# The last four gradient stores of an attention backward pass, each issued as nine transfers over every ninth partition

## The chip, the cores and the metric

The kernel runs on one core of a Trainium2 chip. Its time is device microseconds for one execution of the whole program. The median of the runs before the change is 1698.76 us (three runs, 1698.05 to 1699.05). One more execution was recorded by the hardware profiler; its span, from the first to the last instruction, is 1696.2 us, so the span is 2.6 us shorter than the median time. All sums are made on the profiled execution, and differences are carried over to the median.

## What is computed

The reference runs one decode step of a transformer block forward (attention over a key and value cache, then a gated feed-forward layer) and returns its output and the gradients of all inputs but one. Cut to what matters here:

```
q = (x @ wq) as B=4 batches x H=32 heads x Dh=128
p = softmax(q . k_cache / sqrt(Dh))          # k_cache: 4 x 32 x 4096 x 128
o = p . v_cache
...
dV[b,h] = outer(p[b,h], do[b,h])             # 4096 x 128 for each of the 128 heads
dK[b,h] = outer(ds[b,h], q[b,h])             # the same shape
```

Each head's dK and dV is an outer product of a vector with 4096 elements and one with 128, so there is little arithmetic and much to store: dK and dV are 128 heads x 1 MB each. With the two passes over the caches the page counts 422.59 MB read and 282.34 MB written.

## The kernel before the change

All engines' instruction streams are written out by hand order (`tc.manual_schedule()`, line 98); a framework adds the semaphore waits that the data dependences need. One large SBUF tile, `arena` (line 112), is cut into 23 slots of 4160 bf16 elements in each of the 128 partitions. `Slot` takes one, `Slot2` (line 146) takes two neighbours, enough for a pair of heads, 128 partitions x 8192 elements (16 KB a partition, 2 MB). `give` puts slots back on the list when the transfer that reads them has been issued; the framework makes the next writer wait until that transfer has landed.

The work has three phases: a forward pass over all heads, the feed-forward layer, and the backward pass. In the backward pass the last 96 heads go as 48 pairs (`NT = 48`). For each pair t the loop of line 1476 does the following:

- `load_pairs` (line 1282) loads v for a later pair (line 1280);
- `front_pair` (line 1292) transposes v with TensorE (line 1298), copies it back with ScalarE (line 1299) and multiplies it with do (line 1313);
- `more_V` (line 1395) makes dV of some pair: `P2_pair` on GpSimd (line 1376), then `grad_pair` into `out_3` (line 1414);
- `grad_pair` into `out_2` (line 1489) makes dK of pair t;
- after every second pair `group_dS_pair` (line 1319, with lines 1326 and 1329 on VectorE) makes the ds of the next two.

`grad_pair` (line 1386) takes a slot pair, runs one VectorE product of 128 x 8192 (line 1379), and issues one store of 2 MB from SyncE's queue (line 1389). In DRAM the two heads of a pair are next to each other, and `two_heads` (line 1272) views them as 128 rows of 8192 elements, one for each partition.

All large loads and stores go through SyncE's queue in the order of the program. The framework gives them eight completion semaphores in turn, called lanes here: a transfer waits, before it is issued, until the one eight places earlier in the queue has landed completely. A semaphore counts to 16 for each transfer.

The last four products of the program are, in this order on VectorE: dK of pair 45, dV of pair 47, dK of pair 46, dK of pair 47.

Of the kernel before, what the change touches and what calls it, by code (L numbers as in the profile page):

```python
# [27 lines left out]
def kernel(  # L28
# [22 lines left out]
    nc = tc.nc  # L51
# [6 lines left out]
    Dh = A_k_cache.shape[3]  # L58
# [6 lines left out]
    SJ = Sk // P  # L65
# [142 lines left out]
    for i in range(2):  # L208
        t = fcon.tile([P, 64], BF16, name=f"onesw{i}")
# [4 lines left out]
    def ones_window(col):  # L214
# [11 lines left out]
                          in_=rowg[:, None, :, None].to_broadcast([P, 4, 8, 4]))  # L226
# [738 lines left out]
    with ExitStack() as c2:  # L965
# [297 lines left out]
        NT = (NH - SP) // 2  # L1263
# [8 lines left out]
        def two_heads(ap, t):  # L1272
            b, h = t % B, H0 + t // B * 2
            return ap[b, h:h + 2].rearrange("h (p j) d -> (h p) (j d)", p=P // 2)
# [103 lines left out]
        def outer_pair(dst, col2, row):  # L1378
            nc.vector.tensor_tensor(  # L1379
                out=dst.rearrange("p (j r t) -> p j r t", r=Dh // 2, t=2),  # L1380
                in0=col2[:, :, None, :].to_broadcast([P, 2 * SJ, Dh // 2, 2]),
                in1=row.rearrange("p (r t) -> p r t", t=2)[:, None, :, :].to_broadcast([P, 2 * SJ, Dh // 2, 2]),
                op=ALU.mult,
            )

        def grad_pair(out_ap, t, col2, row):
            g_ = Slot2()
            outer_pair(g_.t[:, 0:2 * SJ * Dh], col2, row)
            nc.sync.dma_start(out=two_heads(out_ap, t), in_=g_.t[:, 0:2 * SJ * Dh])
            g_.give()  # L1390

        O0, S0, S1, L, LP = 2, 21, 35, 5, 3
        gvd = {"n": 2, "t": 0}

        def more_V(upto):
            while gvd["n"] < min(SP, upto):
                s = gvd["n"]
                P_pairs(s)
                replicate("rdo", s - s % REP)
                grad_V(s)  # L1400
                P_pairs(s + 1)
                P_pairs(s + 2)
                gvd["n"] += 1
                if s % REP == 2 and s + 2 < SP:
                    replicate("rdo", s + 2)
                elif s % REP == 2:
                    replicate_pair("rdo", 0)
                if s >= SP - 2:
                    P2_pair(s - SP + 2)
            while gvd["t"] < NT and SP + 2 * gvd["t"] + 2 <= upto:  # L1410
                t = gvd["t"]
                P2_pair(t)
                replicate_pair("rdo", t // B)
                grad_pair(out_3, t, pP2.pop(t), reps["rdo", "p", t // B][:, t % B, :])
                P2_pair(t + 1)
                gvd["t"] += 1
                if t % B == 2:
                    replicate_pair("rdo", t // B + 1)
# [57 lines left out]
        for t in range(NT):  # L1476
            s = SP + 2 * t
            load_pairs(t + LP)
            if t % B == 2:
                replicate_pair("rq", t // B + 1)  # L1480
            if t + LP < NT:
                front_pair(t + LP, lambda: side(s))
            else:
                if t + LP == NT:
                    rows_out()
                    rows_T()
                side(s)
            more_V(s + 2 + lead_V(s))
            grad_pair(out_2, t, pdS[t // 2][:, t % 2], reps["rq", "p", t // B][:, t % B, :])
            if t % 2 == 1 and t + 1 < NT:  # L1490
                group_dS_pair((t + 1) // 2)
            side(s + 1)
# [31 lines left out]
```

## Time and profile before

| | |
|---|---|
| median of 3 runs | 1698.76 us (1698.05 to 1699.05) |
| span of the profiled execution | 1696.2 us |
| busy: TensorE, VectorE, ScalarE, GpSimd | 1233.4, 1234.4, 959.5, 336.9 us |
| moved by DMA | 707.45 MB, mean 417 GB/s |
| stores of line 1389 | 96 of 2048 KB, median 27.9 us from issue to landing |
| last product of VectorE ends | 1666.8 us |
| last store issued | 1666.8 us |
| last store landed | 1694.9 us |

The page gives busy shares of each engine; an engine with a low share is not the bound, and one with a high share need not be it either. The DMA row of the page is the mean busy share of the core's 16 DMA engines in 40 slices of the span, a tenth a digit. A stretch can also be asked for alone; a share of 0.06 there is one engine of sixteen (0.0625). The trace also holds every count of every semaphore, so that it can be seen when each of the engines of one transfer was done.

### The profile page before, as it was taken

The page shows a single profiled execution, that of the slowest core. Times are in us where ns is not written, and L with a number is a line of the kernel's source. Part 1 is how long each engine was busy: PE and PEld are TensorE (multiplying, and loading weights), DVE is VectorE, ACT ScalarE, POOL GpSimd, SP SyncE. Part 2 cuts the span into 40 slices and gives each one's busy share as a digit, 9 for nine tenths or more (in the row PEclk, how much of TensorE's full clock was granted, in tenths as well). Part 3 has the DMA queues.
Part 4 walks back from the last instruction along what each step waited for, and adds up shares of the span by engine and source line. Part 5 has one row for each costly group of instructions (what it writes and reads, how often), then busy time and mean ns, then how long its engine had stood idle before and what let it go on. Part 6 is the DMA issues. An engine that isn't in the chain of part 4 may idle for free.

```text
span 1696.2 us, 37839 instructions
## 1 busy us (share of the span) xinstructions
PE 1233.4 (73%) x16228; PEld 943.4 (56%) x16228; DVE 1234.4 (73%) x1198; ACT 959.5 (57%) x1490; POOL 336.9 (20%) x583
## 2 busy tenths in 40 slices
PE   5889888888888888877876755667665666766650
PEld 4777667666677666655655544444444444444440
DVE  5989999999998997667766466575665655655683
ACT  3555544454454544677665555666665666666650
POOL 1211222222222222222231121011210102011120
PEclk8999999999999999899898689886678777676675
DMA  9999999999999999999999999999999999999995
GB/s 401 424 424 424 424 424 424 424 424 423 416 423 406 424 414 397 395 414 425 425 425 429 428 429 428 429 430 429 429 429 428 418 430 429 422 418 425 415 429 230
DMA packets 81000, 707.45 MB, mean 417 GB/s; under 512 B 8748, under 2 KB 12984, under 8 KB 15296
## 3 DMA queue, kind: packets, MB, share of 16 engines
q1 hardware_dynamic: 80416, 704.94, 99.0%
q8 instruction: 127, 2.08, 0.5%
q14 instruction: 41, 0.34, 0.0%
q0 software_dynamic: 416, 0.10, 0.0%
HBM read 422.59 MB, written 282.34 MB: 416 GB/s over the span
## 4 chain that ended last, share of the span: by engine, by line
DMA 46%; DVE 9%; PE 3%; issue 2%; ACT 1%; DVEq 0%; POOL 0%; SPq 0%; ACTq 0%
DMA out_dram<-arena 43%; DVE arena L1379 7%; DMA arena<-in_A_v_cache_dram 3%; DVE arena L806 1%; PE M_ps L472 1%; DVE arena L457 1%; PE pt_w L601 0%; ACT arena L1299 0%; ACT Pn L436 0%; DVEq L1519 0%; PE kP_ps L482 0%; DVE dPr L1326 0%; PE pt_tps L1298 0%; PE gu_ps L873 0%; PE dn_ps L904 0%
## 5 line engine op out<-in xcount | busy, mean ns | idle before, releaser
L1299 ACT COPY arena<-pt_tps 128x1024 bf16<-128x1024 bf16 x384 | 369.8, 1023 | 232.3 <-PE pt_tps L1298 231.6
L1298 PE MATMUL pt_tps<-ident_b,arena 128*128 128x128 bf16 x3072 | 308.1, 272 | 204.7 <-DMA arena<-in_A_v_cache_dram 149.4
L1298 PEld LDWEIGHTS <-arena 128*128 128x128 bf16 x3072 | 263.9, 125 | 304.2 <-DMA arena<-in_A_v_cache_dram 172.8
L1379 DVE TENSOR_TENSOR arena<-arena 128x8192 bf16<-128x8192 bf16 x48 | 212.5, 4427 | 205.1 <-DMA out_dram<-arena 202.3
L472 PE MATMUL M_ps<-arena 128*128 128x130 bf16 x4096 | 285.1, 222 | 42.9 <-DMA arena<-in_A_v_cache_dram 42.2
L457 DVE TENSOR_TENSOR arena<-arena 128x4096 bf16<-128x4096 bf16 x128 | 292.5, 2285 | 23.9 <-POOL arena L453 23.9
L472 PEld LDWEIGHTS <-arena 128*128 128x128 bf16 x4096 | 251.9, 99 | 64.0 <-DMA arena<-in_A_v_cache_dram 57.2
L1379 DVE TENSOR_TENSOR arena<-dS,arena 128x8192 bf16<-128x8192 bf16 x48 | 212.3, 4424 | 73.0 <-DMA out_dram<-arena 73.0
L364 DVE STREAM_TRANSPOSE arena<-arena 128x512 f32<-128x512 f32 (+1 forms) x321 | 250.7, 797 | 0.0
L359 ACT COPY arena<-pt_tps 128x1024 bf16<-128x1024 bf16 x128 | 129.5, 1012 | 188.9 <-PE pt_tps L358 150.5
L1376 POOL COPY arena<-arena 128x128 bf16<-128x128 bf16 x48 | 55.3, 1153 | 492.3 <-ACT arena L1353 286.3
L370 POOL TENSOR_TENSOR W<-qrep,wmask 128x128 bf16<-128x128 bf16 x128 | 120.2, 939 | 85.6 <-PE S_ps L390 70.8
L801 ACT COPY arena<-pt_tps 128x1024 bf16<-128x1024 bf16 x128 | 121.7, 1025 | 26.1 <-PE pt_tps L800 24.8
L453 POOL COPY arena<-P_all 128x64 bf16<-128x64 bf16 x128 | 32.7, 255 | 412.8 <-ACT P_all L447 409.8
L806 DVE TENSOR_TENSOR arena<-dS,arena 128x4096 bf16<-128x4096 bf16 x32 | 73.2, 2293 | 35.0 <-DMA out_dram<-arena 34.7
L800 PE MATMUL pt_tps<-ident_b,arena 128*128 128x128 bf16 x1024 | 78.5, 229 | 27.1 <-ACT arena L801 27.1
L1313 PE MATMUL dP_ps<-arena 128*32 128x512 bf16 x768 | 85.7, 484 | 7.6 <-ACT arena L1299 7.3
L800 PEld LDWEIGHTS <-arena 128*128 128x128 bf16 x1024 | 67.2, 104 | 37.5 <-issue 35.9
L447 ACT COPY P_all<-pt_P 32x64 bf16<-32x64 bf16 x256 | 52.1, 204 | 53.6 <-PE pt_P L443 51.4
L806 DVE TENSOR_TENSOR arena<-P,arena 128x4096 bf16<-128x4096 bf16 x29 | 66.4, 2295 | 19.8 <-DMA out_dram<-arena 19.8
L358 PE MATMUL pt_tps<-ident_b,arena 128*128 128x128 bf16 x1024 | 80.1, 222 | 0.0
L482 PE MATMUL kP_ps<-arena,onesw 128*32 128x512 bf16 x1024 | 79.6, 388 | 0.0
(245 smaller groups left out, 1576.5 us busy)
## 6 DMA issues: line engine op xcount, KB each, us to landing
out_dram<-arena SPq DMA_DIRECT2D x96, 2048.0 KB, 27.9
arena<-in_A_v_cache_dram SPq DMA_DIRECT2D x160, 1024.0 KB, 15.9
arena<-in_A_k_cache_dram SPq DMA_DIRECT2D x128, 1024.0 KB, 15.3
arena<-in_A_v_cache_dram SPq DMA_DIRECT2D x48, 2048.0 KB, 32.1
out_dram<-arena SPq DMA_DIRECT2D x72, 1024.0 KB, 20.2
arena<-in_A_wq_dram SPq DMA_DIRECT2D x8, 1024.0 KB, 14.4
arena<-in_B_w_dram SPq DMA_DIRECT2D x8, 896.0 KB, 15.3
out_dram<-arena SPq DMA_DIRECT2D x6, 896.0 KB, 28.4
```

Of the source, the lines that this page charges most:

```text
L359: nc.scalar.copy(out=KT[:, c * GW:(c + 1) * GW, :], in_=pt[:])
L364: nc.vector.transpose(out=KT[:, c * w_:(c + n) * w_], in_=Kn[:, c * w_:(c + n) * w_])
L370: nc.gpsimd.tensor_tensor(out=W[:, hl], in0=qrep[:, :, s:s + 1].to_broadcast([P, 4, 32]), in1=wmask[:, hl, None, :].to_broadcast([P, 4, 32 ...
L457: nc.vector.tensor_tensor(out=PK[:, :, 0:Dh].rearrange("p j (r t) -> p j r t", t=2), in0=Ks[s].heads().rearrange("p j (r t) -> p j r t", t=2),
L472: nc.tensor.matmul(hold["M"][:], lhsT=Vn[:, j, :], rhs=PK[:, j, :], start=(j == 0), stop=(j == SJ - 1))
L800: nc.tensor.transpose(pt[:, i, :], v[:, g * GW + i, :], ident_b[:])
L801: nc.scalar.copy(out=v[:, g * GW:(g + 1) * GW, :], in_=pt[:])
L806: nc.vector.tensor_tensor(out=dst.rearrange("p j (r t) -> p j r t", t=2), in0=col2[:, :, None, :].to_broadcast([P, SJ, Dh // 2, 2]), in1=r ...
L1298: nc.tensor.transpose(pt[:, i, :], v[:, g * GW + i, :], ident_b[:])
L1299: nc.scalar.copy(out=v[:, g * GW:(g + 1) * GW, :], in_=pt[:])
L1313: nc.tensor.matmul(rows["acc"][32 * c:32 * (c + 1), :], lhsT=zt[t % B][:, 32 - m:64 - m], rhs=v[:, j0:j0 + 4, :], start=(pl == 0 and u == ...
L1379: nc.vector.tensor_tensor(out=dst.rearrange("p (j r t) -> p j r t", r=Dh // 2, t=2), in0=col2[:, :, None, :].to_broadcast([P, 2 * SJ, Dh / ...
```

## The change

The last four stores of pairs (dK of pairs 45, 46 and 47, dV of pair 47) go through a new function. It issues nine transfers in place of one: the first takes partitions 0, 9, 18 and so on to 126, the second 1, 10, ..., 127, and so on. The first two have 15 partitions, the other seven 14. All other stores are issued as before.

```diff
         def grad_pair(out_ap, t, col2, row):
             g_ = Slot2()
             outer_pair(g_.t[:, 0:2 * SJ * Dh], col2, row)
-            nc.sync.dma_start(out=two_heads(out_ap, t), in_=g_.t[:, 0:2 * SJ * Dh])
+            store_pair(two_heads(out_ap, t), g_.t[:, 0:2 * SJ * Dh], t, out_ap is out_2)
             g_.give()
+
+        def store_pair(dst, src, t, is_k):
+            if t < (NT - 3 if is_k else NT - 1):
+                nc.sync.dma_start(out=dst, in_=src)
+                return
+            for o in range(9):
+                nc.sync.dma_start(out=dst[o::9, :], in_=src[o::9, :])
```

## The prediction

> **What bounds the kernel now.** I read the page first. The DMA row says that the queues carry the whole program, except for the last slice; the chain of work that ended last agrees, since its largest share is stores.
>
> ```profile
> DMA  9999999999999999999999999999999999999995
> GB/s 401 424 424 424 424 424 424 424 424 423 416 423 406 424 414 397 395 414 425 425 425 429 428 429 428 429 430 429 429 429 428 418 430 429 422 418 425 415 429 230
> ...
> DMA 46%; DVE 9%; PE 3%; issue 2%; ACT 1%; DVEq 0%; POOL 0%; SPq 0%; ACTq 0%
> ```
>
> The last slice moves 230 GB/s, so I asked for the busy time of four stretches of it. In the rows below the last two columns are the DMA share and GB/s; the fourth figure with a bracket is VectorE (DVE).
>
> ```profile
> 1655.00:1674.00 19.00, 0.00 (x0) 0.00 (x0) 11.79 (x3) 0.00 (x0) 0.00 (x0) 0.50 1.00 429
> 1674.00:1677.30 3.30, 0.00 (x0) 0.00 (x0) 0.00 (x0) 0.00 (x0) 0.00 (x0) 0.50 0.43 184
> 1677.30:1694.50 17.20, 0.00 (x0) 0.00 (x0) 0.00 (x0) 0.00 (x0) 0.00 (x0) 0.50 0.06 27
> 1694.50:1696.20 1.70, 0.00 (x0) 0.00 (x0) 0.00 (x0) 0.00 (x0) 0.00 (x0) 0.50 0.00 0
> ```
>
> For 17.2 us the share is 0.06, one engine of sixteen: **one DMA engine is 17 us behind the others**, and the program ends with it. The semaphore counts say the same of the last store: fifteen counts from 1674.63 to 1677.61, the sixteenth at 1694.89. The ten transfers before show the same lag (16.7 to 17.3 us). The late engine moves rows of 16 KB in 0.607 us each (27 GB/s); eight rows and a count come to 4.86 us a store, and four stores to 19.5 us.
>
> SyncE's waits and the timeline from 1652 us show what issues those stores.
>
> ```profile
> SPq L1389 <- DVE arena L1379: 564.8, 91, 12.1
> ...
> SPq L1389 <- DMA arena<-in_A_v_cache_dram: 19.5, 13, 4.7
> ```
>
> ```profile
> 1647.70 4.41 DVE L1379 TENSOR_TENSOR arena<-dS,arena 128x8192 bf16<-128x8192 bf16 x1
> 1652.14 15.01 SPq L1389 DMA_DIRECT2D out_dram<-arena  x4
> ...
> 1653.70 4.42 DVE L1379 TENSOR_TENSOR arena<-arena 128x8192 bf16<-128x8192 bf16 x1
> 1658.03 8.75 DVE L1379 TENSOR_TENSOR arena<-dS,arena 128x8192 bf16<-128x8192 bf16 x2
> ```
>
> A store waits mostly for its product, but line 1389 also waits for loads of v, which it does not read: that is the lane, the transfer eight places earlier. The stores here are issued at 1652.14, 1658.14, 1662.52 and 1666.81, each within 0.03 us of its product's end. No lane holds them up, because a transfer of 2 MB takes a lane, and eight lanes (39 us of the late engine's work) are more than the 27 us from issue to landing.
>
> **The change, part by part.**
>
> *Issues.* Four transfers become 36. Two issues of SyncE that follow each other in the trace are 0.38 to 0.80 us apart (median 0.44 over the 142 closest pairs). Taken alone that is 8 x 0.44 = 3.5 us a store, under the 4.4 us of a product, and costs nothing.
>
> *Lanes.* 36 transfers on eight lanes are another matter. Number them 0 to 35. Their lanes are held by the last stores of the old form, whose sixteenth counts came in the trace at 1640.97, 1646.05, 1651.13, 1656.07, 1660.93, 1665.81, 1670.66 and 1675.52. So transfers 0 to 2 go at 1652.1 to 1653.0, and then one each time that the late engine finishes: number 3 at 1656.1, number 7 not before 1675.54. Transfer 8 needs the lane of transfer 0, long free, and goes at 1675.9. The first store, issued at 1652.14 before, is complete in the queue 23.8 us later, and the fifteen engines that were ahead have run dry by then (seven rows in place of 32).
>
> *Products.* In the built program the three products that follow have new waits. Before, they wait for the store that last read their slot, long landed. After the change:
>
> ```
> L1379 TensorTensor arena<-arena 128x8192           [waits DMAHW4,DMAHW3,DMAHW5,DMAHW2,DMAHW6,DMAHW1,DMAHW7,DMAHW0,Pool]
> L1379 TensorTensor arena<-dS_21974,arena 128x8192  [waits DMAHW4,DMAHW3,DMAHW5,DMAHW2,DMAHW6,DMAHW1,DMAHW7,DMAHW0,DVE]
> L1379 TensorTensor arena<-dS_21974,arena 128x8192  [waits DMAHW4,DMAHW5,DMAHW3,DMAHW6,DMAHW2,DMAHW7,DMAHW1,DMAHW0]
> ```
>
> The counts waited for are those after the ninth transfer of the store before. The slots are different ones; the framework seems to take a read of every ninth partition as a read of the whole arena. Whatever its reason, the last three products now each wait until the store in front of them has landed. VectorE has nothing else queued behind them. **Product and store, which overlapped, take turns.**
>
> *The chain.* Its terms:
> - landing of transfer 8 (t1): issue at 1675.92. The first transfers of the program give the lead on an idle engine: issued at 0.74, first packets at 1.77. A first packet took 1.14 where later ones of its size took 0.31, so 0.83 more. With 0.61 for a row and 0.40 from the last count's packet (1694.49) to its arrival (1694.89), transfer 7 starts at 1676.6 and ends at 1678.0, transfer 8 at 1678.65, and it has landed at 1679.0. Without the slow first packet: 1678.2. Taken: 1678.8.
> - landing to product: 0.09 in the trace (landing 1618.52, product 1618.61), 0.17 for the first, where one more wait follows; product 4.42; product to issue 0.03.
> - store of nine transfers on idle engines (d): 1.03 lead, 0 to 0.83 for the first packet, nine rows of 0.613 with the count (5.5), 0.40: 6.95 to 7.8. Issues are no bound at 0.44 (eight in 3.5 us), and the ninth's lane is free after 3 us. At 0.80 an issue d is 6.4 + 1.03 + 0.83 + 0.61 + 0.40 = 9.3. Taken: 7.6, since most issues are near the median.
> - end: 1694.89 to 1696.18, 1.29.
>
> Sum: 1678.8 + (0.17 + 0.09 + 0.09) + 3 x (4.42 + 0.03 + 7.6) + 1.29 = 1716.6, against 1696.2: **20.4 us more**, so 1719.2 for the median of 1698.76. The ends: 1678.2 and d = 6.95 give 1714.0 (+17.8, 1716.6); d = 9.3 gives 1721.7 (+25.5, 1724.3).
>
> *Which engines.* The profile has no transfer of 14 or 15 rows by SyncE, so it does not tell which engines they go to. If the late one gets none, the sum above holds. If it gets its share, it owes transfers 0 to 6 when it is done with the old stores at 1675.0: 9 x 0.613 more to transfer 8, landing at 1680.95 in place of 1678.8, later by 2.2. After that all engines are idle in each turn, and it costs no more. That is +22.6, 1721.4; with the long d, 1726.5. The first transfer's packets start as eight (1.77 to 1.85) and eight (2.32 to 2.39); the last store's counts come as seven (1674.63 to 1674.93), eight (1676.56 to 1677.61) and the late one, so it is the eighth of one batch. That fits the end of a batch, which a transfer of 14 or 15 would leave out first, if engines are taken in order; I lean to spared by a little. The two cases are closer to each other than the ends of d.
>
> The Trainium skill, in "DMA: Bandwidth & Descriptors", section "Why a DMA increments its semaphore by 16 and not by 1", says that a transfer from SyncE runs on the largest count up to 16 that divides the rows, on the lowest-numbered engines: 14 or 15 here, so engine 15 would be spared. "Latency and other measured facts" there says that engines 7 and 15 are usually slower; by it the late one is spared (1719.2) or not (1721.4). The same page's "Rules for kernel authors" speaks against the change: transfers of 128 partitions and 1 MiB or more for bandwidth, with a fixed cost of about 2.0 us each; paid nine times a store without overlap, three stores would by this estimate take 3 x 9 x 2.0 = 54 us of fixed cost alone. The sum here lets eight overlap.
>
> **The rivals.**
>
> 1. *Faster: the late engine is relieved and nothing waits.* Freed of 32 rows it lands at 1675.5; the others get 4 rows more, 1677.3 + 2.4 + 0.4 = 1680.1, and the span is 1681.4, median 1684.0. The idle 17 us above speak for it. Against it are the lane waits, which line 1389 is seen to obey. It decides if the 36 transfers are in the queue by about 1677, as the four are by 1667; by the lanes only some ten are.
> 2. *Same: lanes hold, but products are free.* After 1675.54, 29 rows of 0.613 are left on each engine: 1676.6 + 0 to 0.8 + 17.8 + 0.4 + 1.3 = 1696.1 to 1696.9, median 1698.7 to 1699.5. What the late engine is spared the others lose waiting. The waits quoted speak against it.
> 3. *Much slower: a transfer of 14 or 15 rows uses few engines.* The trace has only stores of 128 rows. On one engine a store is 128 x 0.613 = 78 us, 71 more than 7.6; three in series and the 84 rows of transfers 3 to 8 before them make about 285 us, 1984.
> 4. *That the change does not do what it says* (the late engine gets its share) is the case of +22.6 above.
>
> **How the numbers follow.** Turns with the late engine spared: 0.48. Turns with its share: 0.37. Few engines or another far dearer transfer: 0.07. Rival 2: 0.05. Rival 1: 0.03. A difference of 0.2% (3.4 us) is about what can be told from no change here. Slower is then 0.92, same 0.05, faster 0.03. The likeliest case gives 1719.2. The two cases of turns hold 0.85, and the range takes in their ends, 1716.6 and 1726.5, with 1.5 us for a lag that is not quite that of the profiled run: 1715 to 1728.
>
> **What would show it.** In the profile after: three VectorE products of line 1379 after 1675, each some 12 us after the one before, with the DMA share near zero during each; VectorE's waits for stores longer by about 20 + 2 x 7.6 us; SyncE waiting at the new store's line from 1653 to 1675; the fifteen other engines with a share of about 0.2 between 1658 and 1675. Wrong would be: products at 1653.7, 1658.0 and 1662.4 as before; a store of nine that takes 5 or 10 us and not 7.6; a row that takes other than 0.61 us when only 14 engines run.

## The result and the profile after

After the change the median is **1726.61 us** (four runs, 1726.39 to 1727.15) against 1698.54 us for the kernel before in the same session (four runs, 1698.05 to 1699.05): the ratio is 1.0168, with a 95% interval of 1.0155 to 1.0181. The span of the profiled execution is 1724.7 us, 28.5 us more than before.

The page shows where to look. In the DMA row, 38 of the 40 slices are full as before; the last two have a share of 5 and 3 tenths, with 228 and 146 GB/s in the row below. In the chain of work VectorE has fallen from 9% to 7% and SyncE's issues (SPq) have risen from 0% to 1%.

```profile
DMA  9999999999999999999999999999999999999953
GB/s 401 424 425 424 424 423 424 425 422 423 419 424 408 425 412 397 378 425 424 425 426 428 429 429 428 429 430 429 430 428 427 422 428 430 424 423 424 420 228 146
...
DMA 47%; DVE 7%; ACT 1%; PE 1%; SPq 1%; issue 1%; DVEq 0%
```

The timeline of that stretch has start, duration, engine, line and, in brackets, the idle time before and what ended it.

```profile
1651.93 69.78 SPq L1397 DMA_DIRECT2D out_dram<-arena  x36
...
1682.42 4.42 DVE L1379 TENSOR_TENSOR arena<-arena 128x8192 bf16<-128x8192 bf16 x1 [28.97 <-DMA out_dram<-arena]
1696.14 4.42 DVE L1379 TENSOR_TENSOR arena<-dS,arena 128x8192 bf16<-128x8192 bf16 x1 [9.30 <-DMA out_dram<-arena]
1709.80 4.43 DVE L1379 TENSOR_TENSOR arena<-dS,arena 128x8192 bf16<-128x8192 bf16 x1 [9.23 <-DMA out_dram<-arena]
```

The last three products, which began at 1653.70, 1658.03 and 1662.4 before, now begin at 1682.42, 1696.14 and 1709.80. Each waits for a store out of the arena, from a slot that it does not use. The distance is 13.7 us: 4.42 for the product and 9.2 for the store after it. The last store's last count arrives at 1723.41.

The windows of one stretch in which the lanes hold SyncE, of one product and of one store give the DMA share and GB/s in their last two columns:

```profile
1658.00:1675.00 17.00, 0.00 (x0) 0.00 (x0) 0.00 (x0) 0.00 (x0) 0.00 (x0) 0.50 0.19 73
1682.42:1686.84 4.42, 0.00 (x0) 0.00 (x0) 4.42 (x1) 0.00 (x0) 0.00 (x0) 0.50 0.00 0
1686.87:1696.14 9.27, 0.00 (x0) 0.00 (x0) 0.00 (x0) 0.00 (x0) 0.00 (x0) 0.50 0.54 226
```

The queues carry nothing during a product and little over half of what they can during a store. What fills a store is told by the chain of waits. Its lines have start, duration and holder; the second of the four stores begins like this and ends so:

```profile
1682.42 4.43 DVE arena L1379
...
1686.87 0.81 SPq L1397
1687.68 0.04 issue
1687.72 0.80 SPq L1397
...
1692.72 0.78 SPq L1397
1693.50 0.04 issue
1693.55 2.48 DMA out_dram<-arena
```

Nine issues of SyncE follow each other every 0.83 us, and the chain runs through eight of them; only the ninth transfer's own 2.48 us stands there as DMA. **In a turn the issues are the bound, not the rows.** All 36 issues take 0.77 us and more (median 0.784); the issue of a store of 128 rows took 0.33 before. The two lines that follow have the least, median and greatest duration of the issues in ns, first for the whole stores before, then for the 36:

```profile
L1389 SPq DMA_DIRECT2D out_dram<-arena x96: 332/332/626, 899.1 to 1666.8; - x96
```

```profile
L1397 SPq DMA_DIRECT2D out_dram<-arena x36: 771/784/1328, 1651.9 to 1720.9; - x36
```

A row of 16 KB takes 0.613 to 0.627 us in the turns, which is less than the 0.83 from one issue to the next.

### The profile page after: what moved, and what is told of

Its sections match the earlier page's. It is cut to its first block, busy times and chain, and to the rows that moved or that the text cites. A ratio compares the mean times of both kernels' runs of the same rounds, so it can differ in the third digit from the quotient of the medians.

```text
span 1724.7 us, 37882 instructions
## 1 busy us (share of the span) xinstructions
PE 1246.9 (72%) x16228; PEld 957.5 (56%) x16228; DVE 1234.4 (72%) x1198; ACT 959.9 (56%) x1490; POOL 345.4 (20%) x583
## 4 chain that ended last, share of the span: by engine, by line
DMA 47%; DVE 7%; ACT 1%; PE 1%; SPq 1%; issue 1%; DVEq 0%
DMA out_dram<-arena 38%; DMA arena<-in_A_v_cache_dram 8%; DVE arena L1379 6%; DVE arena L806 1%; SPq L1397 1%; ACT arena L1299 1%; PE pt_tps L1298 1%; ACT arena L801 0%; PE dP_ps L1313 0%; ACT arena L978 0%; PE gps L984 0%; PE dP_ps L1228 0%; DVE dPr L1326 0%; SPq L1280 0%; ACT dPr L1203 0%
## 5 line engine op out<-in xcount | busy, mean ns | idle before, releaser
L1298 PE MATMUL pt_tps<-ident_b,arena 128*128 128x128 bf16 x3072 | 310.8, 274 | 197.2 <-DMA arena<-in_A_v_cache_dram 143.9
L1298 PEld LDWEIGHTS <-arena 128*128 128x128 bf16 x3072 | 266.9, 126 | 296.4 <-DMA arena<-in_A_v_cache_dram 166.8
L472 PEld LDWEIGHTS <-arena 128*128 128x128 bf16 x4096 | 254.4, 99 | 51.5 <-DMA arena<-in_A_v_cache_dram 44.5
L800 PE MATMUL pt_tps<-ident_b,arena 128*128 128x128 bf16 x1024 | 83.9, 239 | 24.7 <-ACT arena L801 24.6
L800 PEld LDWEIGHTS <-arena 128*128 128x128 bf16 x1024 | 72.0, 109 | 35.5 <-issue 34.3
L358 PE MATMUL pt_tps<-ident_b,arena 128*128 128x128 bf16 x1024 | 80.9, 224 | 0.0
L1290 POOL COPY arena<-dOT_bf 128x2 bf16<-128x2 bf16 x48 | 58.9, 1230 | 108.6 <-PE dP_ps L1313 108.5
```

What stands on the lines that cost most here:

```text
L472: nc.tensor.matmul(hold["M"][:], lhsT=Vn[:, j, :], rhs=PK[:, j, :], start=(j == 0), stop=(j == SJ - 1))
L800: nc.tensor.transpose(pt[:, i, :], v[:, g * GW + i, :], ident_b[:])
L1298: nc.tensor.transpose(pt[:, i, :], v[:, g * GW + i, :], ident_b[:])
```

## The experiments

Each is timed beside the kernel before on the same chip, whose medians were 1697.95, 1698.21 and 1698.08 us in three sessions. My theory after the result: the turns are the loss, and within a turn it is the price of an issue. The rivals: the loss lies in the lanes and the late engine before the turns, or in the mere number of transfers, or in the rows.

### Products ahead of the stores

All 36 transfers are kept, but issued after the last product, so that nothing has to take turns.

```diff
-            for o in range(9):
-                nc.sync.dma_start(out=dst[o::9, :], in_=src[o::9, :])
+            late.append((dst, src))
...
+        late_stores()      # the same nine transfers for each of the four, after the last pair
```

> The 36 transfers stay as they are, but are issued after the last product, so that no product waits for a split store. Theory (most of the loss is products and stores taking turns): products end at 1666.8 as before the change; transfer 7 still waits for its lane until about 1675.5, and 28 transfers follow at the 0.83 us an issue that the changed kernel shows: last issue 1698.8, landed 2.5 later, end 1.3 later: span about 1702.6, median about 1705. Rival (the loss is the price of 36 small transfers, the waits of the products cost little): about 1726, as the changed kernel.

Measured: 1707.06 us, ratio 1.0054 (1.0038 to 1.0071). The timeline has the products where they were before the change:

```profile
1653.70 4.42 DVE L1379 TENSOR_TENSOR arena<-arena 128x8192 bf16<-128x8192 bf16 x1
1658.03 8.76 DVE L1379 TENSOR_TENSOR arena<-dS,arena 128x8192 bf16<-128x8192 bf16 x2
1666.93 34.85 SPq L1404 DMA_DIRECT2D out_dram<-arena  x36
```

Without turns 19 of the 28 us are gone (each run against its own session). The 9 that stay come from 36 issues in a row: 35 x 0.83 = 29 of the 34.85 us that SyncE needs for them after the last product. Most of the rest is issues drawn out to as much as 1.9 us between 1669.7 and 1679.5, while the old stores were being finished.

### Turns with whole stores

The reverse: nothing is split, but the last four products share one slot pair, so that each waits for the store in front of it.

```diff
-            g_ = Slot2()
+            last4 = t >= (NT - 3 if out_ap is out_2 else NT - 1)
+            g_ = one["s"] if last4 and one else Slot2()
```

> No store is split; the last four products of the kernel before share one slot pair, so each waits until the store in front of it has landed. Theory (turns alone make most of the loss): the first store lands at 1680.4 as before, then three times 0.1 + 4.42 + 0.03 and a store of 128 rows on idle engines, 1.03 to 1.6 + 0 to 0.83 + 8 x 0.607 + 0.40, about 7.1 us: landed 1715.4, span 1716.7, median about 1719. Rival (nine transfers are what costs): about 1699, as before.

Measured: 1715.45 us, ratio 1.0103 (1.0089 to 1.0117), 3.5 below what I expected. The timeline, and the window of one store:

```profile
1679.78 4.43 DVE L1379 TENSOR_TENSOR arena<-arena 128x8192 bf16<-128x8192 bf16 x1 [26.52 <-DMA out_dram<-arena]
...
1690.58 4.42 DVE L1379 TENSOR_TENSOR arena<-dS,arena 128x8192 bf16<-128x8192 bf16 x1 [6.38 <-DMA out_dram<-arena]
1701.38 4.42 DVE L1379 TENSOR_TENSOR arena<-dS,arena 128x8192 bf16<-128x8192 bf16 x1 [6.37 <-DMA out_dram<-arena]
```

```profile
1684.23:1690.49 6.26, 0.00 (x0) 0.00 (x0) 0.00 (x0) 0.00 (x0) 0.00 (x0) 0.50 0.79 335
```

A whole store lands 6.26 us after its issue on idle engines, one of nine 9.16 us. **This run splits the loss.** Turns alone cost 17.2 us. The split adds 2.5 (first store landed at 1682.20 in place of 1679.69) and 3 x 2.9 = 8.7 for the stores in the turns; together 28.4, against the 28.1 of the medians.

### Only the last store split

```diff
-            if t < (NT - 3 if is_k else NT - 1):
+            if t < NT - 1 or not is_k:
```

> Only the very last store is split in nine; no product comes after it. Theory (turns, not splitting, make the loss): transfers 3 to 7 go as the late engine frees their lanes, the last at 1690.05, the late engine carries nine rows in place of eight: landed 1695.6, span 1696.9, median about 1699.5, which is no difference that can be told. Rival (each split store costs its share of 28 us): about 1705.5.

Measured: 1700.91 us, ratio 1.0017 (1.0008 to 1.0027), 1.4 more than expected. No product follows the split store, so there are no turns. Five of the nine transfers wait for a lane, the late engine is still the last, and 3 us are lost instead of the idle time won. The late engine's last two whole stores come 5.39 and 5.86 us after the one before, where the step was 4.84 before the change, and its nine rows of the split store take 5.87 where eight took 4.84. Rows take up to 1.25 us while the split store runs beside it.

### Eight transfers of sixteen partitions

Fewer transfers, and sixteen rows in each, one for every engine.

```diff
-            for o in range(9):
-                nc.sync.dma_start(out=dst[o::9, :], in_=src[o::9, :])
+            for o in range(8):
+                nc.sync.dma_start(out=dst[o::8, :], in_=src[o::8, :])
```

> Each of the four stores is eight transfers of 16 partitions (every eighth) in place of nine of 14 or 15; the products still wait in turn. Theory (an issue is dear, 0.83 in place of 0.44, because 14 or 15 rows do not go to all sixteen engines): a store takes 1.03 + 0 to 0.83 + 8 x 0.61 + 0.40, about 6.9 us, and the span is 1680.3 + 0.35 + 3 x (4.45 + 6.9) + 1.3 = 1716, median about 1718.5. Rival (any small transfer in a row costs 0.83 to issue): a store takes 7 x 0.83 + 2.5 = 8.3 us, span 1720, median about 1722.7.

Measured: 1734.51 us, ratio 1.0215 (1.02 to 1.023). **Both theories missed**: it is slower than nine. The window of one store:

```profile
1687.66:1699.21 11.55, 0.00 (x0) 0.00 (x0) 0.00 (x0) 0.00 (x0) 0.00 (x0) 0.50 0.80 182
```

Compare it with the same window after the change (share 0.54, 226 GB/s): the engines are busier and move less, because a row takes 1.23 us (median of 128) in place of 0.62. Issues here take 0.49 us where nothing blocks them; so it is the rows. The Trainium skill, "SBUF — State Buffer", section "Door 1: The DMA port swizzle", gives a reason for that figure: four neighbouring partitions, and the four 32 further on, have one of sixteen ports, so that partitions eight apart reach eight ports, two on each. The 1.23 us, twice 0.62, agree. By the same formula fifteen partitions nine apart have fifteen different ports, and with a step of nine the rows in the turns are indeed 0.613 to 0.627 us, none longer. The step also sets how far apart the rows lie in DRAM (128 KB here, 144 KB with nine), and no run separates the two.

### Nine blocks of neighbours

The same nine sizes, but with neighbouring partitions.

```diff
-            for o in range(9):
-                nc.sync.dma_start(out=dst[o::9, :], in_=src[o::9, :])
+            r0 = 0
+            for n in (15, 15, 14, 14, 14, 14, 14, 14, 14):
+                nc.sync.dma_start(out=dst[r0:r0 + n, :], in_=src[r0:r0 + n, :])
+                r0 += n
```

> Nine transfers of 15, 15, 14, ... partitions again, but each of neighbouring partitions in place of every ninth. Theory (the products wait because a read of every ninth partition is taken for a read of the whole arena): the new waits are gone, products end at 1666.8, and the transfers are held by lanes and issues as in the run with the products first: median about 1705. Rival (the turns come with nine transfers a store, whatever their partitions): about 1726. A third outcome: the Trainium skill, in SBUF - State Buffer, section Door 1: The DMA port swizzle, says that partitions share ports by fours, so that a block of 14 reaches about four of sixteen ports; by its 27.2 GB/s a port a transfer would take an estimated 2.1 us in place of 0.6, and the 29 after 1675.5 some 61 us: about 1740.

Measured: 1721.22 us, ratio 1.0136 (1.0121 to 1.0151). The products' rows in the timeline, and the window of the whole end:

```profile
1654.54 4.42 DVE L1379 TENSOR_TENSOR arena<-arena 128x8192 bf16<-128x8192 bf16 x1
1658.87 8.75 DVE L1379 TENSOR_TENSOR arena<-dS,arena 128x8192 bf16<-128x8192 bf16 x2
```

```profile
1678.50:1716.00 37.50, 0.00 (x0) 0.00 (x0) 0.00 (x0) 0.00 (x0) 0.00 (x0) 0.50 0.82 179
```

Two things follow. The products do not wait, so it is the step between partitions that makes the framework order a product behind a store of another slot. And an issue of 14 neighbouring rows that nothing blocks takes 0.32 us, not 0.78, so the step makes the issue dear too. What is won by both is lost in the rows: they take 1.15 us (median), up to 3.9, at 179 GB/s. So none of the three expected times was met. Fourteen neighbours reach four ports by the formula above, from which the expectation had an estimate of 2.1 us a transfer. Here several transfers are in flight on different partitions, and one comes to 1.28 us (14 rows at 179 GB/s); no run has such a transfer alone.

### Steps and counts

One run on what sets the price of an issue: the last store cut into 64 rows two apart, then 16, 15, 14, 8, 7 and 3 rows four apart, then one.

```diff
+                for p0, step, n in ((0, 2, 64), (1, 4, 16), (65, 4, 15), (3, 4, 14), (59, 4, 8), (91, 4, 7), (119, 4, 3), (125, 1, 1)):
+                    p1 = p0 + step * (n - 1) + 1
+                    nc.sync.dma_start(out=dst[p0:p1:step, :], in_=src[p0:p1:step, :])
```

> A look, for the price of an issue and for the late engine's place: only the very last store is cut, into 64 partitions in steps of 2, then 16, 15, 14, 8, 7 and 3 in steps of 4, and one alone. Theory (issue time follows the step between partitions): the five transfers in steps of 4 take the same time to issue, under 0.78, whether they have 16 or 7 rows, and the single one about 0.32. Rival (it follows the rows, dear when they do not fill sixteen engines): 64 and 16 rows at about 0.5, all others at about 0.8. The late engine: the transfer of 8 rows, issued about 1680, either lands within 3 us or waits for the late engine until after 1690; the same for 7, 3 and 1. The smallest that waits gives the late engine's place in the order, and by the Trainium skill's DMA: Bandwidth & Descriptors it would be the eighth or the sixteenth. Median about 1700.

Measured: 1698.21 us in its one run. Durations of the issues that nothing blocked, with those of the other runs:

| rows | step | issue, us |
|---|---|---|
| 128, 119, 14, 4, 1 | none | 0.33, 0.35, 0.32, 0.25, 0.26 |
| 105, 15 | none | 0.41, 0.41 |
| 64 | 2 | 0.60 |
| 8, 7, 3 | 4 | 0.65, 0.72, 0.70 |
| 16 | 8 | 0.49 |
| 15, 14 | 9 | 0.81, 0.78 |

A step costs 0.2 to 0.5 us an issue; the number of rows matters less, and not in one direction. Neither theory names the rule, and I leave it at the table. The issues of 64 rows, and of 105 and 15 without a step, were made while old stores were still in the queues, and may be drawn out by that: the first issue after the change took 0.98 us in that state and 0.81 in the turns. The 16, 15 and 14 rows four apart were drawn out (1.2 us and more) behind the rows ahead of them and say nothing. As for the late engine, the transfers of 8 and 7 rows each have one count 12.8 us or more after the others (1694.83, 1695.43), and that of 3 rows has none.

### Eight transfers without a step, in turns

Turns as in the run with whole stores, and each store in eight transfers of 1024 columns of all 128 partitions: many transfers, no step, no rows crowded on a port.

```diff
+                for o in range(8):
+                    nc.sync.dma_start(out=dst[:, o * 1024:(o + 1) * 1024], in_=src[:, o * 1024:(o + 1) * 1024])
```

> The kernel before, with the last four products in one slot pair (turns, as in the run with whole stores in turns, which took 1715.4 us), and each of the four stores cut into eight transfers by columns: 128 partitions x 1024 elements each, so every engine has work in every transfer and partitions are not stepped. Theory (it is the step of nine between partitions that made a store of nine take 9.2 us; the number of transfers costs little): eight issues at the 0.35 to 0.41 us that neighbouring rows showed are 3.1 us and hide beside the rows, a store takes 6.3 to 7.0 us, products 10.8 to 11.5 us apart, 1715.5 to 1718. Rival (the number of transfers and their lanes made it dear): a store takes about 9 us, products 13.5 us apart, 1724 to 1727, as with nine stepped transfers.

Measured: 1718.60 us, ratio 1.0122 (1.0108 to 1.0135), 0.6 above the theory's range and 5 below the rival's. The timeline:

```profile
1681.62 4.43 DVE L1379 TENSOR_TENSOR arena<-arena 128x8192 bf16<-128x8192 bf16 x1 [27.05 <-DMA out_dram<-arena]
1693.21 4.43 DVE L1379 TENSOR_TENSOR arena<-dS,arena 128x8192 bf16<-128x8192 bf16 x1 [7.16 <-DMA out_dram<-arena]
```

Products are 11.6 us apart, and a store lands 6.81 us after its first issue: 0.55 more than a whole one, where nine stepped transfers take 2.9 more. The number of transfers is not what made a store dear.

### Two queues

If the 0.83 us between issues bounds a turn, two queues should halve it: every other transfer goes through ScalarE's queue.

```diff
-                nc.sync.dma_start(out=dst[o::9, :], in_=src[o::9, :])
+                (nc.scalar if o % 2 else nc.sync).dma_start(out=dst[o::9, :], in_=src[o::9, :])
```

> The changed kernel with every second of the nine transfers issued by ScalarE's queue, which has nothing left to do then. Theory (a store of nine on idle engines takes 9.2 us because SyncE needs 0.83 for each issue, more than the 0.62 of a row): issues alternate, rows bind, a store takes about 7.6 us, three of them 4.7 us less: median about 1721.5. Rival (the rows or the engines bind): no change, about 1726.6.

Measured: 1726.82 us, ratio 1.0168 (1.0155 to 1.0182): **no change, and my theory missed**. The view of the new line has, for each queue, the number of issues, then the least, median and greatest duration in ns, then the first and last start; the window of one store follows:

```profile
L1397 SPq DMA_DIRECT2D out_dram<-arena x20: 774/872/1660, 1660.3 to 1718.8; - x20
L1397 ACTq DMA_DIRECT2D out_dram<-arena x16: 817/1052/1814, 1652.3 to 1717.9; - x16
```

```profile
1688.26:1697.32 9.06, 0.00 (x0) 0.00 (x0) 0.00 (x1) 0.00 (x0) 0.00 (x0) 0.50 0.60 232
```

The issues do run beside each other: the first counts of the transfers of a store are now about 0.6 us apart, which is one row. But then engines are in two transfers at once, rows take up to 1.57 us, the counts of one transfer spread over up to 2.2 us, and the store lands 8.9 us after its first issue, 5.3 after the start of its last one (2.5 with one queue). With one queue the issues are the bound, with two the rows; the two limits lie 0.3 us apart. What three turns gain by this, 0.8 us, is lost before them: the first of the four stores lands at 1683.59, not 1682.20.

### Which engine is late

Three runs leave the kernel before as it is, but for its last store, in neighbouring partitions. The first gives 119 rows to seven engines of 17.

```diff
+            cuts = (0, 119, 126, 128) if out_ap is out_2 and t == NT - 1 else (0, 128)
+            for p0, p1 in zip(cuts, cuts[1:]):
+                nc.sync.dma_start(out=dst[p0:p1, :], in_=src[p0:p1, :])
```

> Only the very last store is cut, into neighbouring partitions: 119, 7 and 2. No product follows. If 119 = 7 x 17 rows go to seven engines in order and the late engine is the eighth, it is spared eight rows, 4.9 us, and the seven others end at about 1674.6 + 11 x 0.61 = 1681: span about 1691.4, median about 1694, faster than before. Rival (the late engine is among the first seven): it carries 18 rows in place of 8, median about 1705. Second rival (119 rows go to one engine): 119 x 0.61 = 73 us, about 1745.

Measured: 1707.60 us, ratio 1.0057 (1.0043 to 1.0071). Six counts of the 119 rows come from 1683.7 to 1685.5 and one at 1704.56: the late engine is among the first seven, and now has 18 rows in place of 8. The second run (`cuts = (0, 105, 113, 119, 124, 128)`) narrows it down:

> The kernel before, with its last store cut into five transfers of neighbouring partitions: 105 (on fifteen engines of 7 rows), 8, 6, 5 and 4. What it is to tell is which engine in the order of the engines is the late one: 7 rows had one count that came 13 us after the others, 3 rows had none, so it is the fourth to the seventh. Each of the transfers of 6, 5 and 4 rows has one count near 1690 to 1695 if the late engine is among its engines, and none after about 1685 if not. If the late engine is the seventh, none of the three has one; the sixth, only 6 rows; the fifth, 6 and 5; the fourth, all three. Issues: theory (the step is what makes an issue dear) 0.32 to 0.42 us each for 8, 6, 5 and 4 rows; rival (few rows make it dear) 0.5 us and more. The late engine keeps 7 + 1 to 4 rows, so the time stays within 0.2% of the kernel before or up to 2 us above it.

Measured: 1701.98 us in one run. The transfers of 6 and 5 rows each have one count that comes 19 to 20 us after their others (1698.49, 1699.10); that of 4 rows has its four counts from 1680.76 to 1681.15. **The late engine is the fifth in the order in which a transfer takes engines.** The one issue of few rows that nothing blocked, of 4 rows without a step, took 0.25 us. The run took 3.9 us more than the kernel before, not up to 2. Two more rows are 1.2 us. The rest is a slower late engine: at 1670.15 it was no later than before the change (1670.66), but the whole store after it came 7.35 us later, at 1677.50, where the step was 4.86 before. In these 7 us the rows of the split store ran beside it.

The third uses it: with 87 rows on three engines of 29, which leaves out the fifth, then 32 and 9, the late engine has 3 rows in place of 8.

> The kernel before, with only its last store cut into three transfers of neighbouring partitions: 87, 32 and 9. By the counts of 119 = 7 engines x 17 rows and of 8, 7 and 3 rows in earlier runs, 87 rows should go to three engines of 29 rows, which are not the late one, 32 to sixteen engines of 2, and 9 to nine engines of one. Theory (the end is set by the one late engine, 17 us behind, and by rows of 0.61 us): the late one then has 3 rows in place of 8, so it ends some 5 x 0.61 = 3.0 us earlier; the three others have 32 rows, 24 more than now, about 14.6 us after 1677.3, so they end near 1692 as well. Median 1695.2 to 1696.5 against 1698.5, ratio about 0.9985. Rival (rows that share a port or the extra transfers take back the gain): 1698 to 1701, ratio 1.000 or more.

Measured: 1698.34 us, ratio 1.0003 (0.9994 to 1.0012): **no gain**. The window of a stretch in which the share was 0.06 before:

```profile
1681.00:1688.00 7.00, 0.00 (x0) 0.00 (x0) 0.00 (x0) 0.00 (x0) 0.00 (x0) 0.50 0.26 73
```

Four engines work, which is 0.25, but at 18 GB/s each, not 27: some rows take up to 2.6 us. The late engine's last three whole stores come 4.85, 5.60 and 7.43 us after each other, so it loses 0.7 + 2.6 = 3.3 us beside the three, and saves 5 x 0.61 = 3.0 us of rows. One of the three is no earlier: its last count comes with the late engine's, 1695.18 and 1695.22, where they were expected near 1692.

## Why the prediction was right, and where it was not

- **Lanes.** Right. From the end of its third issue (1655.1) to 1676.6 SyncE issues one transfer each time that the late engine frees a lane; the queues' share from 1658 to 1675 is 0.19, where "about 0.2" was written.
- **Products that wait, and turns.** Right, and the core of it: moving the stores behind the products takes 19 us away, and turns without any split cost 17.2. VectorE's waits for stores are 47.5 us; the "20 + 2 x 7.6" that was written for them does not fit the prediction's own sum, in which the first product waits from 1653.7 to 1679.0, 25 us.
- **Which engines.** The likeliest case failed here: the late engine is not spared. The order of the counts was read as "the eighth of one batch"; it is the fifth, and gets a row of each transfer. A transfer of 15 has 14 counts close together and a late one (the first: 1655.27 to 1658.87, then 1677.2), and one of 14 has 13 and a late one. The Trainium skill, "DMA: Bandwidth & Descriptors", section "Why a DMA increments its semaphore by 16 and not by 1", names 15 and 14 engines for these sizes, which agrees. Its section "Latency and other measured facts" calls engines 7 and 15 the slower ones; if a transfer takes the lowest-numbered first, the fifth here is neither.
- **The landing of transfer 8.** 1682.20, not 1678.8. Of the 3.4 us, 2.2 are the late engine's share, as the second case had it; the other 1.2 no case had: it is slowed while it finishes the old stores. Its last one comes 5.89 us after the one before, not 4.86, and the lane that the old trace, shifted to this execution, would free at 1675.2 came free at 1676.57. The split store's rows run beside it; why some of them slow it is not shown. The step was up to 7.36 us beside rows eight apart and up to 7.43 beside rows of neighbouring partitions, but at most 4.90 beside rows two and four apart and 4.93 beside transfers by columns.
- **The store of nine (d).** 9.16, not 7.6: three times 1.56 us, 4.7 in the sum, the largest error. The failed step is "issues are no bound at 0.44". The 0.44 was a median over issues of whole partition ranges; none of its rows had a step. The issues measure 0.78 to 0.81 with 0.04 between them, and 8 x 0.83 + 2.5 = 9.1. The bound that was kept for it (9.3 at 0.80) holds. 9.16 is nearer to the 10 that the prediction named as a sign of being wrong than to its 7.6.
- **The rest.** 0.37 for the three turns from landing to product (0.35 was taken), 3 x 4.45, and 1.29 at the end.
- **The fixed cost.** The 54 us that the prediction estimated from the Trainium skill's "DMA: Bandwidth & Descriptors" are not seen: the three stores in the turns take 27.5 us in all, and eight transfers by columns 0.55 us more than one whole store. (The page fits the 2.0 us, under "Anatomy of one DMA", to transfers that GpSimd issues; these are SyncE's.)

With the measured terms, 1682.20 + 0.37 + 3 x (4.45 + 9.16) + 1.29 = 1724.69, the span. The case "its share, with the long d" stood at 1726.5 for the median, as an end of the range, and that is what happened; the likeliest case, 1719.2, was 7.4 us short. That the end is met to 0.1 us is luck: its span was 1723.9, 0.8 short, and the 2.6 us from span to median were too many. In the profiled execution after the change the time is 1.8 us over the span (1726.48 and 1724.7). Rival 1 (relieved) fails by the lanes; rival 2 (products free) is what the run with products ahead comes near, some 8 us above what it said, since issues cost 0.83; rival 3 fails by the counts.

Open: why one engine is 17 us behind at the end of the program. No run tried to change it earlier than in the last four stores. Nor is it settled what in a step makes an issue dear.

## What to carry to other kernels

An imbalance at the end of a program is worth only what a change leaves of the overlap around it: here 17 us of one engine were the target, and turns like those that came with the new access pattern cost 17 us by themselves. Look in the built program at which waits an access pattern adds, before the bytes are counted. When a store is cut into pieces, take the price of an issue from a row with the same step, and see that the pieces in flight do not meet on the same partitions' ports; of the cuts tried here in turns, the one by columns, which keeps all 128 partitions in each piece, costs the least (0.55 us for eight).

## What the runs showed that was not expected

- An issue from SyncE costs 0.25 to 0.41 us without a step between partitions and 0.49 to 0.81 with one.
- A row of 16 KB takes 0.61 us alone, and 1.23 us with partitions eight apart; 1.15 us (up to 3.9) in neighbouring blocks. A high DMA share can thus stand beside a low rate: 0.80 with 182 GB/s, where before 1.00 was 429.
- The engine that ends late is the fifth in order in this kernel. It lags 16 to 18 us behind on the old stores, not the same in each execution, and up to 20 us once split stores run beside them.
